# The first half product of the experts' first multiplication, passed on in PSUM

## The chip, the core and the metric

The kernel runs on one core of a Trainium2 chip. The metric is device time in microseconds (us). Five engines take part: TensorE (PE, with its weight loads PEld in a row of their own), VectorE (DVE), ScalarE (ACT), GpSimd (POOL) and SyncE (SP), which issues transfers. Each engine runs its own instructions in the order in which they were written for it, and waits where an operand is not ready.

## The reference, cut to what matters

```python
x = attention(q, k, v, phi)                # 4 x 8 x 576 x 64, as [2304, 512]
h = x @ w_in;  x = (h * cos(h)) @ w_out    # [512, 2048], [2048, 512]
p = domain_probs / (domain_probs.sum(-1, keepdims=True) + 1e-09)
out = 0
for e in range(4):
    h = maximum(x @ w1[e], 0.0)            # [2304, 512] @ [512, 1024]
    out += p[:, e:e+1] * (h @ w2[e])       # [2304, 1024] @ [1024, 512]
```

All values are 32-bit floats. The change touches the product `x @ w1[e]` in the last loop.

## The kernel before, in words

The kernel has two stages. The first (to about 374 us of the profiled execution) computes attention and the product with `w_in` and `w_out`; its order is written out word by word in a plan. The second stage is the loop over experts. It takes the 2304 tokens in two halves, the weights in 16 slices of 256 columns of `w1` (four per expert), and each half's 1152 tokens in two sub-blocks, of 2 x 256 and 2 x 320 tokens. That makes 64 units, one after the other: half by half, within a half slice by slice, within a slice the two sub-blocks.

Every number is held as a sum of a high and a low part, and a product of two such numbers takes three products on TensorE (`mm3`): high by high, high by low, low by high. All products are recorded under line L342.

**A unit's first multiplication** (`hidden`). The block `x @ w1` is a 2 x 2 by 2 x 2 block multiplication done with seven block products instead of eight (in the manner of Strassen and Winograd). The mixed blocks of x are made by `build_x`, once for each half and sub-block: DVE or POOL forms sums and differences in `sA`, `sB` and `acc` (line L390), ACT copies them into the high part (`x<-sB`, line L373), DVE or POOL forms the low part. The mixed blocks of `w1` lie in `wa`. Each of the seven products is six instructions on TensorE, `hp<-x,wa`, 256 or 320 columns wide. They go into three PSUM banks, `px`, `py` and `pz`, all named `hp` in the profile:

- the first product goes into `px`, the fifth into `py`, the second into `pz`;
- ACT copies `px` to SBUF as `p1` (named `p` in the profile, `p<-hp`), and DVE adds `pz` and `p1` into `c` (`c<-hp,p`, line L1089): the first quarter of the result;
- the sixth product adds itself onto `px`, ACT copies it as `u2`; the seventh adds itself, ACT copies it as `u3` (both are `u<-hp` in the profile); the fourth adds itself: the second quarter;
- DVE adds `py` and `u3` into `c`: the third quarter. The third product adds itself onto `py`, and DVE adds `py` and `u2`: the last quarter.

So the sixth product waits for the copy `p1`, the seventh for `u2`, the fourth for `u3`.

**The relu** (`rectify`) reads `px` and `c` with ACT, and writes `c` or a tile `ht` (`h`, `hg` or `hx` in the profile, whose low part DVE makes, L1092). **A unit's second multiplication** takes tokens in tiles of 128, most of them in pairs (`pair_prep`, `pair_out`), the others singly (`one_prep`, `plain_out`). POOL or DVE mix the relu's result in `sm`, ACT copies it into `h7` (the high part). The products `op<-wb,h` and `op<-wt,h` go into two banks `op` for a pair, three instructions of 256 columns each. After the first and the sixth product of a pair DVE gathers (`acc<-op,p_all`, lines L1101 and L1103: weighted by p, added to the output in `acc`); the next product adds itself onto the same bank and waits for the gather. In the second half the first of these gathers of a pair is a copy `ev` on ACT, added to `acc` by POOL or DVE.

**Banks.** `px`, `py` and `pz` come from a ring of four PSUM banks (`p`); `op` comes from another of four (`po`). A unit gives `pz` back after the sum `c<-hp,p`, `px` after the relu, `py` after the last sum. Units 0 and 1 take `pz` from the ring `po`.

**The order.** All steps of the second stage are generators; a list scheduler (`Order.run`) holds estimated times for every engine and hands out the next instruction by estimated start and rank. An instruction's place on its engine is thus decided by estimates when the kernel is written, and the engine keeps to it.

## Time and profile before

| what | value |
|---|---|
| three runs | 1119.89, 1120.53, 1120.99 us; median 1120.53 |
| span of the profiled execution | 1118.8 us |
| from that span to the median of the runs | 1.7 us |
| TensorE busy | 1109.8 us, 99% |
| VectorE busy | 879.0 us, 79% |
| ScalarE busy | 583.7 us, 52% |
| GpSimd busy | 668.5 us, 60% |

The span runs from the first to the last instruction of one profiled execution; the runs' times are taken from outside and hold a little more. A busy share says how long an engine worked, not whether anything waited for it. A row of the timeline has the start, the time from the first start to the last end, engine, line, operation, output and inputs, partitions by elements, and how many instructions were merged (x); what stands in brackets is idle time ahead of it and what ended that. Matmuls overlap: the next one starts before the one ahead has ended, so a group's pace is read from start to start.

### The profile page before, as it was taken

What the parts mean: (1) busy time and instruction counts of PE and PEld (TensorE: products, weight loads), DVE (VectorE), ACT (ScalarE), POOL (GpSimd) and SP (SyncE); (2) the same over time, 40 slices, a digit from 0 to 9 for tenths busy, and PEclk for the clock granted to TensorE, in tenths of its full rate; (3) what the DMA queues carried; (4) which work ended last, traced back from release to release, by engine and by line L of the source; (5) the groups of instructions that cost most, each with busy time, mean ns of one, the idle gap of its engine ahead of it and who ended that gap; (6) DMA issues with size and microseconds to landing.
All of it is one profiled execution on the core that took longest, in us unless ns stands there. A gap on an engine that the chain in (4) does not pass through costs nothing.

```text
span 1118.8 us, 22424 instructions
## 1 busy us (share of the span) xinstructions
PE 1109.8 (99%) x8698; PEld 1055.6 (94%) x8698; DVE 879.0 (79%) x1619; ACT 583.7 (52%) x1219; POOL 668.5 (60%) x1001
## 2 busy tenths in 40 slices
PE   9899999999999999999999999999999999999998
PEld 8689999999999989999999999989999999999997
DVE  5888988898888765777888888778777777777776
ACT  4887766565655424444444543445455545554543
POOL 1455556665677404665767664217587877777774
PEclk9999999999999999999999999999999999999999
DMA  9940636167614037443566456683554345434532
GB/s 305 359 137 25 213 129 228 57 227 266 254 39 180 1 118 250 161 161 114 186 253 237 181 181 232 247 337 130 191 205 174 142 167 214 185 142 154 215 131 86
DMA packets 44299, 201.76 MB, mean 180 GB/s; under 512 B 6176, under 2 KB 15392, under 8 KB 29984
## 3 DMA queue, kind: packets, MB, share of 16 engines
q1 hardware_dynamic: 44192, 200.33, 49.1%
q8 instruction: 68, 1.11, 0.4%
q14 instruction: 39, 0.32, 0.1%
HBM read 132.68 MB, written 67.63 MB: 179 GB/s over the span
## 4 chain that ended last, share of the span: by engine, by line
PE 97%; DMA 1%; DVE 1%; SPq 0%; ACT 0%; issue 0%
PE op L342 52%; PE hp L342 41%; DMA q<-in_qt_dram 1%; PE vw_ps L629 1%; PE warm L765 1%; PE kvp L513 1%; PE spare L757 1%; PE sc L566 0%; SPq L370 0%; PE pe L487 0%; DVE st L576 0%; PE pkt L535 0%; DVE sA L390 0%; ACT u L373 0%; DVE stT L596 0%
## 5 line engine op out<-in xcount | busy, mean ns | idle before, releaser
L342 PE MATMUL hp<-x,wa 128*128 128x320 f32 (+1 forms) x2688 | 405.7, 296 | 0.7 <-ACT u L373 0.5
L1103 DVE SCALAR_TENSOR_TENSOR acc<-op,p_all,acc 128x256 f32<-128x256 f32 (+1 forms) x566 | 301.9, 566 | 121.6 <-PE op L342 117.3
L342 PEld LDWEIGHTS hp<-x,wa 128*128 128x128 f32 x2688 | 373.6, 188 | 5.7 <-ACT u L373 1.2
L342 PE MATMUL op<-gt,wo 128*128 128x288 f32 x1536 | 218.1, 296 | 0.0
L342 PEld LDWEIGHTS op<-gt,wo 128*128 128x128 f32 x1536 | 208.1, 188 | 4.5 <-issue 2.4
L390 POOL TENSOR_TENSOR sm<-c 128x128 f32<-128x128 f32 x180 | 88.2, 496 | 157.6 <-ACT c L373 156.5
L342 PE MATMUL op<-wb,h 128*128 128x256 f32 (+1 forms) x786 | 144.7, 298 | 0.0
L342 PE MATMUL op<-wt,h 128*128 128x256 f32 x888 | 143.3, 281 | 0.0
L373 ACT ACTIVATE u<-hp 128x320 f32<-128x320 f32 (+1 forms) x128 | 52.6, 411 | 154.3 <-PE hp L342 154.3
L342 PEld LDWEIGHTS op<-wt,h 128*128 128x128 f32 x888 | 124.7, 189 | 2.4
L342 PEld LDWEIGHTS op<-wb,h 128*128 128x128 f32 x786 | 116.8, 189 | 3.9
L342 PE MATMUL op<-wb,hg 128*128 128x512 f32 (+1 forms) x477 | 115.5, 385 | 0.0
L342 PE MATMUL hp<-attnT,vw 128*128 128x288 f32 x768 | 113.2, 296 | 0.2 <-DVE attnT L390 0.2
L342 PEld LDWEIGHTS hp<-attnT,vw 128*128 128x128 f32 x768 | 105.2, 188 | 3.5 <-issue 1.6
L390 POOL TENSOR_TENSOR gt<-y,gt 128x576 fp32r<-128x576 f32 x41 | 60.0, 1463 | 79.1 <-ACT gt L373 74.7
L342 PEld LDWEIGHTS op<-wb,hg 128*128 128x128 f32 x477 | 84.8, 188 | 15.5
L736 DVE TENSOR_TENSOR acc<-op,acc 128x576 f32<-128x576 f32 (+1 forms) x120 | 84.7, 710 | 18.6 <-PE op L342 17.3
L390 POOL TENSOR_TENSOR h<-c,h 128x128 fp32r<-128x128 f32 (+1 forms) x140 | 84.3, 621 | 15.8 <-ACT h L373 15.8
L1089 DVE TENSOR_TENSOR c<-hp,u 128x320 f32<-128x320 f32 (+1 forms) x128 | 57.9, 452 | 33.5 <-PE hp L342 24.5
L373 ACT ACTIVATE kk<-hp 128x576 int32<-128x576 f32 x64 | 41.6, 650 | 45.2 <-PE hp L342 45.0
L373 ACT ACTIVATE h<-sm 128x512 fp32r<-128x512 f32 x74 | 46.6, 629 | 34.4 <-POOL sm L390 34.3
L373 ACT ACTIVATE c<-c 128x256 f32<-128x256 f32 (+1 forms) x138 | 55.2, 434 | 14.9 <-DVE c L1089 14.9
(144 smaller groups left out, 1644.8 us busy)
## 6 DMA issues: line engine op xcount, KB each, us to landing
wa<-wa_d SPq DMA_DIRECT2D x21, 1792.0 KB, 8.7
wa_d<-wa SPq DMA_DIRECT2D x16, 1792.0 KB, 10.3
wt<-wt_d SPq DMA_DIRECT2D x21, 1024.0 KB, 4.9
wb<-wb_d SPq DMA_DIRECT2D x21, 1024.0 KB, 7.0
raw<-in_w_dram SPq DMA_DIRECT2D x32, 512.0 KB, 4.9
wt_d<-wt SPq DMA_DIRECT2D x16, 1024.0 KB, 7.3
wb_d<-wb SPq DMA_DIRECT2D x16, 1024.0 KB, 6.7
kv<-in_kv_dram SPq DMA_DIRECT2D x16, 512.0 KB, 7.9
```

Source lines behind the costliest of these rows:

```text
L342: nc.tensor.matmul(out=ps, lhsT=lt(a), rhs=rt(b), start=first and i == 0, stop=last and i == 2, skip_group_check=more,)
L373: return Op("ACT", ns, fn or (lambda: nc.scalar.activation(out=out, in_=in_, func=func, **kw)), *deps, table=table)
L390: eng.tensor_tensor(out=out, in0=in0, in1=in1, op=op)
L513: nc.tensor.matmul(out=kvp[32 * i:32 * i + 32], lhsT=es[:n, c, 32 * i:32 * i + 32], rhs=kv[i // 2][0][0][:, c, i % 2] if c < NC else kv[i ...
L629: nc.tensor.matmul(out=ps[32 * i:32 * i + 32, g, j * FS:j * FS + FS], lhsT=kvT[b][64 * g:64 * g + 64, 1, i, :], rhs=wi[s][0][64 * g:64 * g ...
L736: e = yield dve(155 + 301 * nd, lambda: nc.vector.tensor_tensor(out=dst, in0=op[:, :, :TH], in1=dst, op=ALU.add), o)
L757: nc.tensor.matmul(out=bank, lhsT=ones, rhs=ones, start=True, stop=True, skip_group_check=True)
L765: nc.tensor.matmul(out=warm[:, :128], lhsT=ones, rhs=ones, start=True, stop=True)
L1089: return dve(157 + 1.045 * n, lambda: nc.vector.tensor_tensor(out=out, in0=ps, in1=sb, op=ALU.add), *deps)
L1103: nc.vector.scalar_tensor_tensor(out=dst, in0=ps, scalar=pe, in1=dst, op0=ALU.mult, op1=ALU.add)
```

## The change

In 61 of the 64 units (all but those listed in `PLAIN_SUM`) ACT copies `px` into a PSUM bank of its own, `z`, in place of the SBUF tile `p1`. The second product then adds itself onto that copy (`more=True` leaves out the clearing of the bank), after the sixth. DVE's sum is gone, and the relu reads `z`. The ring `p` has three banks instead of four, and `z` is one bank with a ring of its own. Units 0 and 1 still take `pz` from `po`, unit 2 from `z` now. The diff:

```diff
@@ -138,8 +138,9 @@
 FIRST = "00 01 10 11 02 12 03 13".split()
 PAIRS = ((0,), (1,), (2, 3), (4, 5), (6, 7))
 RINGS = dict(phi=3, kv=4, q=4, raw=2, wi=2, wf=1, wo=2, es=2, st=2, stT=1, kvs=1, vw=2, y=2, kk=1, gt=3, h=2, o=2, c=2,
-             p2=2, raw2=2, tt=1, wa=2, wb=2, wt=2, cq=2, p1=2, u2=2, u3=1, ht0=1, ht1=1, h7=4, h7a=2, h7f=3, h1a=1, sma=2, h1=1, sm=2, p=4, po=4, ev=4, eva=2)
+             p2=2, raw2=2, tt=1, wa=2, wb=2, wt=2, cq=2, p1=2, u2=2, u3=1, ht0=1, ht1=1, h7=4, h7a=2, h7f=3, h1a=1, sma=2, h1=1, sm=2, p=3, z=1, po=4, ev=4, eva=2)
 HALVES = (0,)
+PLAIN_SUM = (0, 1, 2)
 MERGED = ()
 PATIENCE = ({"PE": 0.2, "ACT": 0.5, "DVE": 0.5, "POOL": 0.5, "SP": 0.5, "X": 0.0},
             {"PE": 0, "ACT": 0, "DVE": 0, "POOL": 0.5, "SP": 0.5, "X": 0.0},
@@ -1054,7 +1055,8 @@
     h_ctx = ExitStack()
     h_p = [h_ctx.enter_context(tc.tile_pool(name="hg", bufs=1, reuse_waits="tile"))]
     p_ctx.close()
-    ps_p = ctx.enter_context(tc.tile_pool(name="ps_p", bufs=4, space=PSUM, reuse_waits="tile"))
+    ps_p = ctx.enter_context(tc.tile_pool(name="ps_p", bufs=3, space=PSUM, reuse_waits="tile"))
+    ps_z = ctx.enter_context(tc.tile_pool(name="ps_z", bufs=1, space=PSUM, reuse_waits="tile"))
     ps_q = ctx.enter_context(tc.tile_pool(name="ps_q", bufs=4, space=PSUM, reuse_waits="tile"))
 
     PROD = {1: (0, 0), 2: (1, 1), 3: (2, 2), 4: (6, 3), 5: (3, 4), 6: (4, 5), 7: (5, 6)}
@@ -1252,6 +1254,10 @@
             return pe(6 * max(0.4545 * n + 0.5, 119.5), 130, prod(bank, i_, more), *deps)
 
         def bank(ring="p"):
+            if ring == "z":
+                if not zs:
+                    zs.append(ps_z.tile([128, 512], F32, tag="z", name="z", bufs=1))
+                return zs[0]
             return (ps_p if ring == "p" else ps_q).tile([128, 512], F32, tag="p" if ring == "p" else "q", name="hp")
 
         def kept(tag):
@@ -1264,18 +1270,24 @@
         ky, t0 = yield R["p"]
         py = bank()
         o5 = yield mm(py, 5, t0)
-        k1, t1 = yield R["p1"]
-        p1 = kept("p1")
-        a1 = yield a_(n, p1, px[:, :n], ACTF.Copy, o1, t1)
-        rz = "po" if i < 2 else "p"
+        rz = "po" if i < PLAIN_SUM[-1] else "z"
         kz, t0 = yield R[rz]
         pz = bank(rz)
         todo.set(("H?", i), None)
-        o2 = yield mm(pz, 2, t0)
-        o6 = yield mm(px, 6, a1, more=True)
-        c11 = yield sum_(n, c[:, 0, :n], pz[:, :n], p1, o2, a1, tc_)
-        R[rz].give(kz, c11)
-        R["p1"].give(k1, c11)
+        if i in PLAIN_SUM:
+            k1, t1 = yield R["p1"]
+            p1 = kept("p1")
+            a1 = yield a_(n, p1, px[:, :n], ACTF.Copy, o1, t1)
+            o2 = yield mm(pz, 2, t0)
+            o6 = yield mm(px, 6, a1, more=True)
+            c11 = yield sum_(n, c[:, 0, :n], pz[:, :n], p1, o2, a1, tc_)
+            R[rz].give(kz, c11)
+            R["p1"].give(k1, c11)
+            pz = None
+        else:
+            a1 = yield a_(n, pz[:, :n], px[:, :n], ACTF.Copy, o1, t0)
+            o6 = yield mm(px, 6, a1, more=True)
+            c11 = yield mm(pz, 2, a1, more=True)
         k2, t1 = yield R["u2"]
         u2 = kept("u2")
         a2 = yield a_(n, u2, px[:, :n], ACTF.Copy, o6, t1)
@@ -1287,7 +1299,7 @@
         c22 = yield sum_(n, c[:, 1, n:], py[:, :n], u3, o5, a3, tc_)
         R["u3"].give(k3, c22)
         last = pe(6 * max(0.4545 * n + 0.5, 119.5), 130, prod(py, 3, True), c22)
-        mids[i] = c, kc, px, kx, py, ky, u2, k2, a2, o4, c11, c22, last, tc_
+        mids[i] = c, kc, px, kx, py, ky, pz, kz, u2, k2, a2, o4, c11, c22, last, tc_
         todo.set(("mid", i), None)
         o3 = yield last
         todo.set(("H", i), o3)
@@ -1298,14 +1310,17 @@
         u, s, j = units[i]
         n = SUBS[j][1]
         yield have(("mid", i))
-        c, kc, px, kx, py, ky, u2, k2, a2, o4, c11, c22, o3, tc_ = mids.pop(i)
+        c, kc, px, kx, py, ky, pz, kz, u2, k2, a2, o4, c11, c22, o3, tc_ = mids.pop(i)
+        top = c[:, 0, :n] if pz is None else pz[:, :n]
         if mode(i) != "whole":
             r = yield a_(n, c[:, 0, n:], px[:, :n], ACTF.Relu, o4, tc_)
             R["p"].give(kx, r)
             r2 = yield a_(n, c[:, 1, n:], c[:, 1, n:], ACTF.Relu, c22)
             cs_[i] = c, kc
             todo.set(("c", i, 1), Join([r, r2]))
-            r3 = yield a_(n, c[:, 0, :n], c[:, 0, :n], ACTF.Relu, c11)
+            r3 = yield a_(n, c[:, 0, :n], top, ACTF.Relu, c11, tc_)
+            if pz is not None:
+                R["z"].give(kz, r3)
             yield have(("H", i))
             c12 = yield sum_(n, c[:, 1, :n], py[:, :n], u2, o3, a2, tc_)
             R["u2"].give(k2, c12)
@@ -1317,6 +1332,9 @@
         if through:
             r = yield a_(n, c[:, 0, n:], px[:, :n], ACTF.Relu, o4, tc_)
             R["p"].give(kx, r)
+            if pz is not None:
+                c11 = yield a_(n, c[:, 0, :n], top, ACTF.Relu, c11, tc_)
+                R["z"].give(kz, c11)
             yield have(("H", i))
             c12 = yield sum_(n, c[:, 1, :n], py[:, :n], u2, o3, a2, tc_)
             R["u2"].give(k2, c12)
@@ -1346,8 +1364,10 @@
         h = yield a_(n, ht[:, 0, 0, n:2 * n], px[:, :n], ACTF.Relu, o4, th)
         l1 = yield low_(n, ht[:, 1, 0, n:2 * n], px[:, :n], ht[:, 0, 0, n:2 * n], h, psum=True)
         R["p"].give(kx, l1)
-        h = yield a_(n, ht[:, 0, 0, :n], c[:, 0, :n], ACTF.Relu, c11, th)
-        l2 = yield low_(n, ht[:, 1, 0, :n], c[:, 0, :n], ht[:, 0, 0, :n], h)
+        h = yield a_(n, ht[:, 0, 0, :n], top, ACTF.Relu, c11, th)
+        l2 = yield low_(n, ht[:, 1, 0, :n], top, ht[:, 0, 0, :n], h, psum=pz is not None)
+        if pz is not None:
+            R["z"].give(kz, l2)
         yield have(("H", i))
         c12 = yield sum_(n, c[:, 1, :n], py[:, :n], u2, o3, a2, tc_)
         R["u2"].give(k2, c12)
```

The line numbers of the changed kernel are one higher in the first stage's code and two or more higher behind it (L342 is L343 there, L1103 is L1105). By instruction, TensorE has as many products as before, DVE 54 instructions fewer, ACT 2 more, POOL 7 fewer. The order is the same through the whole first stage.

**Place A, the first two units of the second stage.** These are TensorE's instructions from unit 0's second product on, before. `hp_5014`, `hp_5031` and `hp_5040` are unit 0's `px`, `py` and `pz`; `hp_5042`, `hp_5065` and `hp_5084` are unit 1's; `wa_3732` and `wa_3931` are their slices.

```order
L342 MATMUL hp_5040<-x_4709,wa_3732 128x256 x6
L342 MATMUL hp_5014<-x_4708,wa_3732 128x256 x6
L342 MATMUL hp_5042<-x_4708,wa_3931 128x256 x6
L342 MATMUL hp_5065<-x_4710,wa_3931 128x256 x6
L342 MATMUL hp_5014<-x_4711,wa_3732 128x256 x6
L342 MATMUL hp_5084<-x_4709,wa_3931 128x256 x6
L342 MATMUL hp_5042<-x_4708,wa_3931 128x256 x6
L342 MATMUL hp_5014<-x_4712,wa_3732 128x256 x6
L342 MATMUL hp_5031<-x_4709,wa_3732 128x256 x6
L342 MATMUL hp_5042<-x_4711,wa_3931 128x256 x6
L342 MATMUL hp_5042<-x_4712,wa_3931 128x256 x6
L342 MATMUL op_5142<-wb_4223,hg_5109 128x512 x6
```

And the same place in the changed kernel, where the six names are `hp_5017`, `hp_5034`, `hp_5041`, `hp_5044`, `hp_5099` and `hp_5110`.

```order
L343 MATMUL hp_5041<-x_4709,wa_3732 128x256 x6
L343 MATMUL hp_5017<-x_4708,wa_3732 128x256 x6
L343 MATMUL hp_5044<-x_4708,wa_3931 128x256 x6
L343 MATMUL hp_5017<-x_4711,wa_3732 128x256 x6
L343 MATMUL hp_5017<-x_4712,wa_3732 128x256 x6
L343 MATMUL hp_5034<-x_4709,wa_3732 128x256 x6
L343 MATMUL hp_5099<-x_4710,wa_3931 128x256 x6
L343 MATMUL hp_5110<-x_4709,wa_3931 128x256 x6
L343 MATMUL hp_5044<-x_4708,wa_3931 128x256 x6
L343 MATMUL op_5122<-wb_4223,hg_5088 128x512 x6
```

Unit 0's sixth, seventh and fourth product moved ahead of unit 1's fifth and second; and unit 1's fifth and second stand behind unit 0's last product. ACT's instructions of this stretch, before:

```order
L373 ACTIVATE p1_5038<-hp_5014 128x256
L373 ACTIVATE u2_5058<-hp_5014 128x256
L373 ACTIVATE x_5020<-sB_5023 128x640
L373 ACTIVATE p1_5074<-hp_5042 128x256
L373 ACTIVATE u3_5082<-hp_5014 128x256
L373 ACTIVATE x_5019<-sA_5022 128x640
```

And in the changed kernel:

```order
L374 ACTIVATE p1_5042<-hp_5017 128x256
L374 ACTIVATE u2_5061<-hp_5017 128x256
L374 ACTIVATE x_5023<-sB_5026 128x640
L374 ACTIVATE u3_5076<-hp_5017 128x256
L374 ACTIVATE x_5022<-sA_5025 128x640
L374 ACTIVATE hg_5088<-hp_5017 128x256
```

The copy `u3` of unit 0 stands directly behind the copy of `x` from `sB`, where unit 1's copy `p1` stood before.

**Place B, a single tile's products between two units.** These are TensorE's instructions before; `hp_5438` is a unit's `px`, `hp_5520` its `pz`, and `op_5541` and `op_5542` belong to a tile of the first unit.

```order
L342 MATMUL hp_5485<-x_5019,wa_5276 128x320 x6
L342 MATMUL hp_5520<-x_5016,wa_5276 128x320 x6
L342 MATMUL hp_5438<-x_5020,wa_5276 128x320 x6
L342 MATMUL op_5541<-wb_5406,hg_5109 128x256 x3
L342 MATMUL op_5542<-wb_5406,hg_5109 128x256 x3
L342 MATMUL op_5542<-wt_5194,hg_5109 128x256 x3
L342 MATMUL hp_5438<-x_5021,wa_5276 128x320 x6
```

And in the changed kernel, with `hp_5431` for the `px` and `z_5213` for the bank `z`.

```order
L343 MATMUL hp_5476<-x_5022,wa_5279 128x320 x6
L343 MATMUL hp_5431<-x_5023,wa_5279 128x320 x6
L343 MATMUL z_5213<-x_5019,wa_5279 128x320 x6
L343 MATMUL op_5537<-wb_5407,hg_5088 128x256 x3
L343 MATMUL hp_5431<-x_5024,wa_5279 128x320 x6
L343 MATMUL op_5538<-wb_5407,hg_5088 128x256 x3
L343 MATMUL op_5538<-wt_5217,hg_5088 128x256 x3
```

The second product moved behind the product of `px` that it stood ahead of, and the next product of `px` stands one `op` product earlier.

**Place D, the first pairs of the second half.** TensorE's instructions before; `op_9403` is a pair's first bank, `hp_9469` a `px`, `hp_9488` a `py`, `hp_9501` a `pz`.

```order
L342 MATMUL op_9347<-wt_8962,h7_9306 128x256 x3
L342 MATMUL op_9348<-wb_9213,h7_9306 128x256 x3
L342 MATMUL op_9403<-wt_8962,h7_9325 128x256 x2
L342 MATMUL op_9403<-wt_8962,h7_9326 128x256
L342 MATMUL hp_9469<-x_9176,wa_9077 128x320 x6
L342 MATMUL hp_9488<-x_9180,wa_9077 128x320 x6
L342 MATMUL hp_9501<-x_9177,wa_9077 128x320 x6
L342 MATMUL op_9403<-wt_8962,h7_9325 128x256 x2
L342 MATMUL op_9403<-wt_8962,h7_9326 128x256
L342 MATMUL hp_9469<-x_9181,wa_9077 128x320 x6
```

In the changed kernel at the same pair, whose banks are `op_9328` and `op_9329` here; `op_9274` and `op_9275` are those of the pair ahead, `op_9400` and `op_9401` those of the first pair whose first gather is a copy `ev`, and `hp_9426` is the next unit's `px`.

```order
L343 MATMUL op_9275<-wb_9130,h7_9217 128x256 x3
L343 MATMUL op_9328<-wt_8892,h7_9242 128x256 x2
L343 MATMUL op_9328<-wt_8892,h7_9243 128x256
L343 MATMUL op_9328<-wt_8892,h7_9242 128x256 x2
L343 MATMUL op_9328<-wt_8892,h7_9243 128x256
L343 MATMUL op_9329<-wb_9130,h7_9242 128x256 x2
L343 MATMUL op_9329<-wb_9130,h7_9243 128x256
L343 MATMUL op_9400<-wb_9278,h7_9354 128x256 x3
L343 MATMUL op_9401<-wb_9278,h7_9354 128x256 x3
L343 MATMUL op_9401<-wt_8897,h7_9354 128x256 x3
L343 MATMUL op_9400<-wt_8897,h7_9354 128x256 x3
L343 MATMUL hp_9426<-x_9100,wa_8988 128x320 x6
```

The hp products that stood between a pair's first product and the next one on the same bank have gone from there. DVE's gathers that these products wait for, and what follows them there, in the changed kernel:

```order
L1103 TENSOR_SCALAR acc_70<-op_9328,p_all_78 128x256
L1103 TENSOR_SCALAR acc_70<-op_9274,p_all_78 128x256
L1105 SCALAR_TENSOR_TENSOR acc_70<-op_9275,p_all_78,acc_70 128x512
L1103 TENSOR_SCALAR acc_70<-op_9328,p_all_78 128x256
L1105 SCALAR_TENSOR_TENSOR acc_70<-op_9329,p_all_78,acc_70 128x256
L1103 TENSOR_SCALAR acc_70<-op_9328,p_all_78 128x256
L1105 SCALAR_TENSOR_TENSOR acc_70<-op_9329,p_all_78,acc_70 128x512
L391 TENSOR_TENSOR x_9101<-acc_70,x_9101 128x640
L391 TENSOR_TENSOR sB_9108<-acc_70,sB_9108 128x640
```

The two instructions of `build_x` (`x_9101` and `sB_9108`) stand behind all gathers of that pair. On ACT before, around the first copy `ev`:

```order
L373 ACTIVATE h7_9474<-c_9253 128x256
L373 ACTIVATE h7_9474<-c_9253 128x128
L373 ACTIVATE h7_9474<-sm_9305 128x512
L373 ACTIVATE u2_9526<-hp_9469 128x320
L373 ACTIVATE ev_9534<-op_9511,p_all_78 128x256
L373 ACTIVATE u3_9562<-hp_9469 128x320
```

And in the changed kernel:

```order
L374 ACTIVATE h7_9374<-c_9161 128x256
L374 ACTIVATE h7_9374<-c_9161 128x128
L374 ACTIVATE h7_9374<-sm_9216 128x512
L374 ACTIVATE x_9102<-sB_9108 128x640
L374 ACTIVATE ev_9427<-op_9400,p_all_78 128x256
L374 ACTIVATE z_5213<-hp_9426 128x320
```

Between the copies `h7` and the copy `ev` there now stands the copy of `x_9102` from `sB_9108`, and the copy into `z` stands behind `ev`.

## Rows read from the trace of the kernel before

**Rows 1.** Busy time, share of the span and instructions by engine (the page).

```profile
PE 1109.8 (99%) x8698; PEld 1055.6 (94%) x8698; DVE 879.0 (79%) x1619; ACT 583.7 (52%) x1219; POOL 668.5 (60%) x1001
```

**Rows 2.** Idle time of TensorE's weight loads by releaser: us, times, longest.

```profile
PEld hp L342 <- ACT u L373: 1.2, 3, 0.7
```

**Rows 3.** Timeline of TensorE, last stage: start, duration, rows merged (x).

```profile
904.26 1.60 PE L342 MATMUL hp<-x,wa 128*128 128x256 f32 x12
905.70 0.52 PE L342 MATMUL op<-wt,h 128*128 128x256 f32 x3
```

**Rows 4.** Timeline of TensorE around its four late spots, second stage.

```profile
383.82 4.85 PE L342 MATMUL hp<-x,wa 128*128 128x256 f32 x36
389.14 0.97 PE L342 MATMUL hp<-x,wa 128*128 128x256 f32 x6 [0.47 <-ACT u L373]
...
437.44 0.52 PE L342 MATMUL op<-wt,hg 128*128 128x256 f32 x3
437.90 1.15 PE L342 MATMUL hp<-x,wa 128*128 128x320 f32 x6
...
760.63 0.51 PE L342 MATMUL op<-wb,h 128*128 128x256 f32 x3
761.26 0.98 PE L342 MATMUL hp<-x,wa 128*128 128x256 f32 x6
...
1104.81 1.71 PE L342 MATMUL op<-wt,h 128*128 128x256 f32 x12
1106.36 0.52 PE L342 MATMUL op<-wb,h 128*128 128x256 f32 x3
```

**Rows 5.** Groups of instructions: the removed sum and the copy before it.

```profile
L1089 DVE TENSOR_TENSOR c<-hp,p 128x256 f32<-128x256 f32 (+1 forms) x64 | 28.7, 448 | 6.0 <-PE hp L342 5.2 <-issue 0.3 <-POOL hx L390 0.2
L373 ACT ACTIVATE p<-hp 128x256 f32<-128x256 f32 (+1 forms) x64 | 25.6, 400 | 29.1 <-PE hp L342 29.1
```

**Rows 6.** Timeline of all engines at the start of the second stage.

```profile
380.94 7.72 PE L342 MATMUL hp<-x,wa 128*128 128x256 f32 x60
383.62 0.81 DVE L390 TENSOR_TENSOR sB<-sA,acc 128x640 f32<-128x640 f32 x1
384.47 0.74 ACT L373 ACTIVATE x<-sB 128x640 fp32r<-128x640 f32 x1 [1.50 <-DVE sB L390]
385.11 0.36 ACT L373 ACTIVATE p<-hp 128x256 f32<-128x256 f32 x1
387.27 0.38 ACT L373 ACTIVATE hg<-hp 128x256 fp32r<-128x256 f32 x1 [0.34 <-PE hp L342]
387.68 0.42 DVE L1092 SCALAR_TENSOR_TENSOR hg<-hp,hg 128x256 fp32r<-128x256 f32 x1 [0.22 <-ACT hg L373]
```

**Rows 7.** Timeline of ACT ahead of the late spot at 437.9.

```profile
436.90 0.63 ACT L373 ACTIVATE h<-sm 128x512 fp32r<-128x512 f32 x1 [2.65 <-POOL sm L390]
437.44 0.42 ACT L373 ACTIVATE u<-hp 128x320 f32<-128x320 f32 x1
```

**Rows 8.** Timeline of TensorE and DVE, end of the first half's units.

```profile
720.79 4.60 PE L342 MATMUL hp<-x,wa 128*128 128x320 f32 x30
725.23 1.56 PE L342 MATMUL op<-wb,hx 128*128 128x512 f32 x6
721.66 0.41 DVE L1092 SCALAR_TENSOR_TENSOR hx<-hp,hx 128x256 fp32r<-128x256 f32 x1
```

**Rows 9.** Timeline of DVE and ACT where the second half's units begin.

```profile
766.93 0.48 DVE L1101 TENSOR_SCALAR acc<-op,p_all 128x256 f32<-128x256 f32 x1
767.32 0.74 DVE L1103 SCALAR_TENSOR_TENSOR acc<-op,p_all,acc 128x512 f32<-128x512 f32 x1
764.96 0.73 ACT L373 ACTIVATE x<-sB 128x640 fp32r<-128x640 f32 x1
771.51 0.47 ACT L373 ACTIVATE ev<-op,p_all 128x256 f32<-128x256 f32 x1
```

More of the change, by code (lines that the diff above doesn't have):

```diff
@@ L1359, in rectify @@
         todo.set(("ht", i), Join([l1, l2, l3]))
-    mids = {}
+    mids, zs = {}, []
     cs_, hts, hx, hg, sma, mixed, full = {}, {}, [], [], [], [], []
```

## The prediction

> **What bounds the kernel now.** I read the busy shares first: TensorE works 99% of the span, DVE 79%, ACT 52% [rows 1]. So nothing that lightens DVE or ACT shortens the run by itself; only TensorE's lost time counts. Next I looked for what TensorE loses in the second stage, which is all the change touches. The list of waits shows its weight loads idle 1.2 us in three waits for a copy `u`, the longest 0.7 [rows 2], and no larger wait for this stage's products. The timeline gives the pace: twelve 256-column products take 1.44 us, 0.12 each [rows 3], thirty 320-column ones 4.44, 0.148 each [rows 8]. Against that pace four spots are late [rows 4]: 36 products from 383.82 to 389.14 take 5.32 instead of 4.32 (1.0 lost), the three at 437.44 take 0.46 instead of 0.36, the three at 760.63 take 0.63, the twelve at 1104.81 take 1.55 instead of 1.44. Behind a wait the next six lose 0.1 more (0.97 and 0.98 long where twelve take 1.60, so six 0.88). Together: 1.1 + 0.2 + 0.37 + 0.1, some 1.8 us. That is all the second stage can give back, 0.16% of the time. What the change is worth is therefore decided by the waits that its new order makes.
>
> **The change, part by part.** The sum `c<-hp,p` costs DVE 448 ns [rows 5]; 61 of 64 go, 27.3 us of DVE. It stands beside TensorE's work (no late spot names it), so it is worth nothing directly. The copy stays, 61 times, but into PSUM. No row shows ACT writing PSUM; the nearest is the same copy into SBUF, 400 ns [rows 5], and I take that. From below: shorter gains nothing, as the copy is covered. From above: with 0.1 more it is late only where no more than six 256-column products (0.72) stand between the first product and the sixth, three places, at 0.2 each: 0.6. The Trainium skill (ScalarE: Activation LUTs, Step-by-step: what each stage is for) says that ScalarE reaches PSUM sooner than SBUF; no run here shows that yet, and by it the upper end falls away and the sum below stays. TensorE's number of products is the same, and a second product that adds itself is like the sixth and seventh, which already do. The relu then reads the bank instead of `c`, one ACT pass as before.
>
> What costs is the order. The second product no longer stands between the fifth and the sixth, and a unit has three rotating banks and `z` instead of four rotating ones. I went through the waits of TensorE in the new order and priced each by rows. A copy that ends is followed by its product 0.04 later (437.44 + 0.42 = 437.86, product at 437.90) [rows 4, 7].
>
> Place A, start of the stage. Sixty hp products run in one piece from 380.94 [rows 6]. In the new order the fifth group of six is unit 0's fourth product, wanted at 380.94 + 24 x 0.12 = 383.82. It needs `u3`, and on ACT `u3` stands right behind the copy of x from `sB`, where `p` stood. That copy waits for DVE's `sB` (383.62, 0.81 long) and starts at 384.47; the copy behind it starts at 385.11 and ends 385.47 [rows 6]. DVE's order up to `sB` is unchanged. So the product starts at 385.51, 1.69 late. The third product follows at 386.23 but needs a DVE sum that stands behind the 0.81 subtraction of x: about 386.45, 0.25 late. Unit 1's fifth product now needs unit 0's bank: the copy `hg<-hp` and DVE's subtraction take 0.83 from start to end (387.27 to 388.10 [rows 6]) after the fourth product, with another x subtraction between: 0.3 late. With 0.1 behind each: 2.5 us, where 1.1 were lost: +1.4 (0.5 to 2.0).
>
> Place B, the spot at 437.90. The seventh product there waits for a `u` copy that stands on ACT behind `h<-sm` (436.90), itself waiting for POOL [rows 7]. ACT's order there is the same, but six 256-column products (0.72) move behind the seventh product. It is wanted at 437.08 and starts at 437.90: 0.82 + 0.1, where 0.2 were lost: +0.7 (0.3 to 0.8).
>
> Place C, the first half's last units. The second group of the thirty products from 720.79, at 721.68, is a fifth product; with three rotating banks it needs the bank that DVE's `hx<-hp` reads until 721.66 + 0.41 = 722.07 [rows 8]. It starts at 722.11: 0.43 + 0.1, +0.5 (0 to 0.8). Before, the third group needed that bank, at 722.57.
>
> Place D, where the second half's units begin. Before, three groups of hp stand between the products of a pair; in the new order the pair products follow one another, each waiting for a gather on DVE. Count from the start of the op_9328 products that open the new TensorE excerpt's second row. DVE's first gather of its excerpt is done by then. A 256-wide gather lasts 0.48 and the next starts 0.39 after it, a 512-wide one lasts 0.74 [rows 9]. So gather 2 starts at -0.13, the wide one at 0.26, gather 4 at 0.93, done 1.41. TensorE wants it at 0.36 and starts at 1.45: 1.09 late. The next gather ends at 1.9, TensorE asks at 1.81: 0.1 late. Nine products more to 3.37, then one needs the copy `ev`. DVE has two more gathers, x (0.81 like `sB`) and `sB` to 4.64; ACT copies x from `sB` (0.73) to 5.41 and only then `ev` (0.47) [rows 6, 9]: 5.88. So 2.5 late. Together 3.7 + 0.3, where 0.37 were lost: +3.6 (1.0 to 5.0: from below the `ev` wait gone, from above one gather and one subtraction more ahead of it). Queued behind `ev` on ACT is the copy into `z`, wanted a microsecond later.
>
> Place E: six times in the last 290 us a pair product follows its gather with only six 256-column products between. Such a place cost 0.11 at 1104.81 [rows 4]; six less the one that goes: +0.6 (0 to 0.8).
>
> Sum: 1.4 + 0.7 + 0.5 + 3.6 + 0.6 = 6.8 us, bounds 1.8 to 9.4 (10.0 with the copies' 0.6). The profiled execution spans 1118.8; 1.7 us lie around it up to the median of 1120.5. On the span that gives 1125.6, on the median 1127.3. Where DVE's 27.3 us go: into idle time. The last products and gathers stand as before, so the end costs the same. Every load of x and weights keeps at least 7 us of products, at the pace above, between itself and its use.
>
> **The rivals.** *No change.* DVE, lighter by 61 sums, reaches the two `sB` mixes sooner than its order says. Decisive at D: `sB` must end 2.5 us earlier, before TensorE asks for `ev`. Then A and D lose what they lost before and B, C, E remain: 1.8 us, 1122.3, inside 0.2% (2.2 us). For it speaks DVE's share; against it, that at A no sum is gone yet (units 0 and 1 keep theirs) and at D gathers fill the queue. *Faster.* All 1.8 us of today's late spots vanish: 1118.7, still within 0.2%; more would have to come from outside the stage. *Bank bound.* Place C repeats in every one of the 61 units, 0.43 each: 26 us, 1146.8. In the steady stage the new order leaves 2 us of products or more, at the pace above, between the last reader's release and the bank's next product, which speaks against it. The Trainium skill (Perfetto Trace Analysis, Optimizing Tensor Performance, Matmuls) asks that independent groups of products rotate through different banks, so that one's evacuation overlaps the next; by that rule three banks in place of four cost time. The trace agrees at place C alone, with 0.43.
>
> **How the numbers follow.** My sum 0.77, no change 0.15, faster 0.03, bank bound 0.05. A measurement of this kernel tells 0.2%, 2.2 us, from nothing. The predicted time is 1127.3. The range reaches from the no-change case, 1121.9, to the upper bound 1120.5 + 9.4 = 1129.9; about 0.12 is left out below and above. Slower 0.81 (0.77 and 0.05, less 0.01 for a sum at its lowest bounds), same 0.15, faster 0.04.
>
> **What would show it.** In the changed profile: TensorE's weight loads idle several us on `u`, `ev`, gathers and `hg`, against 1.2; a wait of 1.7 near 384, 0.8 near 437, 0.4 near 722, 1.1 and 2.5 near 770; copies into `z` of 0.36 to 0.44; DVE's busy time some 20 us less. If the waits near 770 are missing, D is wrong, most likely because DVE's order there runs ahead. If hp waits for `z` or a bank in the steady stage, the bank rival holds.

## The result, and the profile after

The changed kernel takes 1130.66 us, the median of four runs (1129.58 to 1132.98), where the kernel before took 1120.76 beside it: a ratio of 1.0092, with a 95% interval from 1.0079 to 1.0105. That is 9.9 us more. The prediction said 1127.3 and slower, with a range to 1129.9: the direction was right, the time lies 0.8 us above the range.

The profiled execution spans 1127.3 us. The page's first part, which answers to [rows 1]:

```profile
PE 1113.7 (99%) x8698; PEld 1057.9 (94%) x8698; DVE 857.4 (76%) x1565; ACT 586.8 (52%) x1221; POOL 659.3 (58%) x994
```

DVE is busy 21.6 us less, TensorE's busy time has grown by 3.9 although it has the same 8698 instructions: some of them are recorded as longer. The list of waits of TensorE's weight loads answers to [rows 2] (us in total, times, longest):

```profile
PEld op L343 <- ACT ev L374: 3.3, 1, 3.3
PEld hp L343 <- ACT u L374: 2.6, 2, 1.7
PEld op L343 <- DVE acc L1103: 1.0, 1, 1.0
PEld hp L343 <- DVE hx L1094: 0.6, 1, 0.6
```

Before there was one row of this size in the stage, 1.2 us, for `u`. Now one wait for `ev` alone takes 3.3. The timeline shows the five places of the prediction in order of time; compare the start of a row with the start of the one ahead plus its number of instructions at full pace (0.12 for 256 columns, 0.147 for 320).

```profile
380.05 3.05 PE L343 MATMUL hp<-x,wa 128*128 128x256 f32 x24
384.64 4.41 PE L343 MATMUL hp<-x,wa 128*128 128x256 f32 x30 [1.53 <-ACT u L374]
...
383.58 0.74 ACT L374 ACTIVATE x<-sB 128x640 fp32r<-128x640 f32 x1 [1.51 <-DVE sB L391]
384.22 0.36 ACT L374 ACTIVATE u<-hp 128x256 f32<-128x256 f32 x1
...
437.10 0.51 PE L343 MATMUL op<-wb,hg 128*128 128x256 f32 x3
438.26 1.15 PE L343 MATMUL hp<-x,wa 128*128 128x320 f32 x6 [0.65 <-ACT u L374]
...
722.15 1.05 PE L343 MATMUL hp<-x,wa 128*128 128x320 f32 x6
723.49 1.74 PE L343 MATMUL hp<-x,wa 128*128 128x320 f32 x10 [0.29 <-DVE hx L1094]
...
768.67 0.62 PE L343 MATMUL op<-wt,h 128*128 128x256 f32 x3
770.11 0.62 PE L343 MATMUL op<-wt,h 128*128 128x256 f32 x3 [0.82 <-DVE acc L1103]
771.79 0.52 PE L343 MATMUL op<-wt,h 128*128 128x256 f32 x3
771.96 1.54 DVE L391 TENSOR_TENSOR x<-acc,x 128x640 fp32r<-128x640 f32 x1
773.43 0.81 DVE L391 TENSOR_TENSOR sB<-acc,sB 128x640 f32<-128x640 f32 x1
774.27 0.74 ACT L374 ACTIVATE x<-sB 128x640 fp32r<-128x640 f32 x1 [1.20 <-DVE sB L391]
774.91 0.46 ACT L374 ACTIVATE ev<-op,p_all 128x256 f32<-128x256 f32 x1
775.42 0.62 PE L343 MATMUL op<-wt,h 128*128 128x256 f32 x3 [3.12 <-ACT ev L374]
775.88 3.00 PE L343 MATMUL hp<-x,wa 128*128 128x320 f32 x12
778.67 0.84 PE L343 MATMUL op<-wt,h 128*128 128x256 f32 x3
...
844.46 0.88 PE L343 MATMUL hp<-x,wa 128*128 128x256 f32 x6
845.22 0.62 PE L343 MATMUL op<-wt,h 128*128 128x256 f32 x3
```

At A 24 products from 380.05 should end at 382.93 by pace, and the next starts at 384.64: 1.71 late, as worked out (1.69). The two ACT rows show why: the copy `u` stands behind the copy of x, whose start waited for `sB`. At B the product follows 1.16 after a group of 0.36: 0.80 late. At C it is 1.34 after a group of 0.88: 0.46 late. At D the gather costs 1.44 - 0.36 = 1.08, with the 0.1 that products lose behind a wait (the fill), and the wait for `ev` 775.42 - 771.79 - 0.36 = 3.27. At E a group of six takes 0.76 where 0.72 is the pace, 0.15 with the fill behind it, and this stands six times.

Behind the wait for `ev` the next rows are slow themselves: twelve products of 320 columns from 775.88 to 778.67 take 2.79, not 1.76. The view by stretches, with its heading (PEclk is the granted clock as a share of full speed), shows it:

```profile
core 0: us, PE busy (x) PEld busy (x) DVE busy (x) ACT busy (x) POOL busy (x), PEclk, DMA share, GB/s
771.50:775.50 4.00, 0.89 (x8) 0.68 (x7) 3.53 (x5) 1.73 (x3) 1.38 (x5) 1.00 0.01 4
775.50:780.00 4.50, 4.50 (x22) 4.50 (x23) 2.81 (x6) 0.42 (x1) 0.96 (x1) 0.62 0.00 0
780.00:784.00 4.00, 4.00 (x31) 4.00 (x31) 1.33 (x4) 1.35 (x3) 0.00 (x0) 1.00 0.00 0
```

TensorE worked 0.89 of the 4 us before; then its granted clock is 0.62 on the mean of 4.5 us, a stretch at the lower level (1.2 GHz; a product of 320 columns follows the one ahead by 0.267 there) and the rest at 2.4. By 780 it is back at 1.00. Counted start to start, the products there take 1.5 us more than at full pace.

The new copy answers to [rows 5]:

```profile
L374 ACT ACTIVATE z<-hp 128x320 f32<-128x320 f32 x31 | 13.1, 422 | 37.6 <-PE hp L343 35.9 <-DVE hx L1094 1.7
L374 ACT ACTIVATE z<-hp 128x256 f32<-128x256 f32 x30 | 11.0, 367 | 13.7 <-PE hp L343 9.0 <-DVE hg L1094 4.7
```

The copy into PSUM takes 422 and 367 ns (320 and 256 columns). The old copy into SBUF took 430 and 369 in the same view of the kernel before. The 400 ns of the prediction were right. The Trainium skill (ScalarE: Activation LUTs, Step-by-step: what each stage is for) says that ScalarE reaches PSUM sooner than SBUF; here that is worth 2 to 8 ns, so by the measurement it doesn't matter in this kernel.

### The profile page after: what moved, and what is told of

The parts are those of the page before. It is cut to its first block, busy times and chain, and to the rows that moved or that the text cites. A ratio compares the mean times of both kernels' runs of the same rounds, so it can differ in the third digit from the quotient of the medians.

```text
span 1127.3 us, 22364 instructions
## 1 busy us (share of the span) xinstructions
PE 1113.7 (99%) x8698; PEld 1057.9 (94%) x8698; DVE 857.4 (76%) x1565; ACT 586.8 (52%) x1221; POOL 659.3 (58%) x994
## 4 chain that ended last, share of the span: by engine, by line
PE 96%; DMA 2%; DVE 1%; SPq 0%; ACT 0%; POOL 0%; issue 0%; POOLq 0%
PE op L343 52%; PE hp L343 36%; PE z L343 4%; PE vw_ps L630 1%; DMA kv<-in_kv_dram 1%; DMA q<-in_qt_dram 1%; PE warm L766 1%; PE kvp L514 1%; SPq L371 0%; PE sc L567 0%; DVE x L391 0%; DVE acc L1105 0%; PE spare L758 0%; POOL hg L391 0%; DVE sB L391 0%
## 5 line engine op out<-in xcount | busy, mean ns | idle before, releaser
L1105 DVE SCALAR_TENSOR_TENSOR acc<-op,p_all,acc 128x256 f32<-128x256 f32 (+1 forms) x566 | 302.9, 568 | 141.0 <-PE op L343 138.2
L343 PE MATMUL hp<-x,wa 128*128 128x256 f32 (+1 forms) x2316 | 356.0, 297 | 2.6 <-ACT u L374 2.2
L343 PEld LDWEIGHTS hp<-x,wa 128*128 128x128 f32 x2316 | 324.1, 189 | 7.3 <-ACT u L374 2.6
L343 PE MATMUL op<-gt,wo 128*128 128x288 f32 x1536 | 218.1, 296 | 0.0
L343 PEld LDWEIGHTS op<-gt,wo 128*128 128x128 f32 x1536 | 208.1, 188 | 4.6 <-issue 2.4
L391 POOL TENSOR_TENSOR sm<-c 128x128 f32<-128x128 f32 x180 | 85.4, 478 | 181.6 <-ACT c L374 181.5
L343 PE MATMUL op<-wt,h 128*128 128x256 f32 x888 | 143.0, 282 | 3.9 <-ACT ev L374 3.1
L343 PE MATMUL op<-wb,h 128*128 128x256 f32 (+1 forms) x786 | 141.3, 299 | 0.0
L343 PEld LDWEIGHTS op<-wt,h 128*128 128x128 f32 x888 | 124.3, 189 | 7.5 <-ACT ev L374 3.3
L343 PEld LDWEIGHTS op<-wb,h 128*128 128x128 f32 x786 | 114.9, 189 | 3.9
L343 PE MATMUL op<-wb,hg 128*128 128x512 f32 (+1 forms) x477 | 115.1, 385 | 0.0
L343 PE MATMUL hp<-attnT,vw 128*128 128x288 f32 x768 | 113.2, 296 | 0.3 <-DVE attnT L391 0.3
L343 PEld LDWEIGHTS hp<-attnT,vw 128*128 128x128 f32 x768 | 105.1, 188 | 3.5 <-issue 1.6
L343 PEld LDWEIGHTS op<-wb,hg 128*128 128x128 f32 x477 | 85.3, 188 | 15.9
L684 DVE SCALAR_TENSOR_TENSOR y<-hp,kk 128x576 f32<-128x576 f32 x64 | 48.1, 751 | 16.7 <-ACT kk L374 16.3
```

The lines of the kernel that those rows point to most:

```text
L343: nc.tensor.matmul(out=ps, lhsT=lt(a), rhs=rt(b), start=first and i == 0, stop=last and i == 2, skip_group_check=more,)
L391: eng.tensor_tensor(out=out, in0=in0, in1=in1, op=op)
L684: o = yield dve(750, lambda: nc.vector.scalar_tensor_tensor(out=y, in0=hv, scalar=0.25, in1=kk, op0=ALU.add, op1=ALU.subtract), o, t0)
L1105: nc.vector.scalar_tensor_tensor(out=dst, in0=ps, scalar=pe, in1=dst, op0=ALU.mult, op1=ALU.add)
```

## Where the time went

From the first product of the second stage to the last one's start it is 739.83 us before (374.72 to 1114.55) and 749.30 after (373.82 to 1123.12): 9.47 more. Counted from start to start, with what the next products lose behind each wait:

| place | before | after | more | predicted |
|---|---|---|---|---|
| A, 380 to 389 | 1.10 | 2.36 | 1.26 | 1.4 |
| B, 437 | 0.21 | 0.92 | 0.71 | 0.7 |
| C, 722 | 0 | 0.56 | 0.56 | 0.5 |
| D, waits at 761 and 768 to 776 | 0.38 | 4.73 | 4.35 | 3.6 |
| D, products at the lower clock | 0 | 1.53 | 1.53 | none |
| E, six gathers | 0.10 | 0.88 | 0.78 | 0.6 |
| four other spots of 0.07 to 0.09 | 0 | 0.31 | 0.31 | none |
| sum | 1.8 | 11.3 | 9.5 | 6.8 |

The runs add 0.5 us outside the span: those of the changed kernel take 2.25 us more than their spans, those of before 1.79. The first stage, whose order is the same, took 0.9 us less in this profiled execution; among the eight profiles of this document whose clock did not fall in it the second stage starts between 372.9 and 374.9, and no cause was looked for. Nor was one for the four other spots.

## The experiments

The theory is that only the new order costs time, at places A to E and by the clock behind D. Its rival is that the arithmetic (the copy into PSUM, the product that adds itself onto it, a bank fewer) costs in every unit. To part them, the order that the scheduler had made was written out as a list and followed word for word, so that arithmetic and order could be exchanged.

**The new order with the old sums (e1).** In the 61 units:

```diff
-            a1 = yield a_(n, pz[:, :n], px[:, :n], ACTF.Copy, o1, t0)
+            a1 = yield a_(n, p1, px[:, :n], ACTF.Copy, o1, t1)
             o6 = yield mm(px, 6, a1, more=True)
-            c11 = yield mm(pz, 2, a1, more=True)
+            o2 = yield mm(pz, 2, t0)
...
+    def add_up(i):
...
+        o = yield sum_(n, c[:, 0, :n], pz[:, :n], p1, o2, a1, tc_)
```

The sum is a step of its own (`add_up`), so that the written-out list can place it on DVE; `...` stands for lines left out.

> The order of the changed kernel on every engine, its three rotating banks and its one bank z, but the old arithmetic: ACT copies the first product to SBUF, the second product clears its bank, and DVE adds the two (61 sums come back, placed on DVE where their product ends). Theory (only the order of the instructions, the waits at A to E and the clock behind D, makes the change slower): the same waits stand, 1130.7 us, ratio 1.0092, within 0.0015. Rival (the copy into PSUM and the product that adds itself onto it cost time in each of 61 units, 0.16 us each): 1120.8 to 1122, ratio under 1.0015.

Measured: 1135.12 us, ratio 1.0136 (1.0123 to 1.0149). Its waits:

```profile
PEld hp L547 <- DVE c L1295: 3.9, 7, 0.7
PEld op L547 <- ACT ev L578: 2.9, 1, 2.9
PEld hp L547 <- ACT u L578: 2.6, 2, 1.7
PEld op L547 <- DVE acc L1309: 2.0, 4, 1.0
```

The waits for `u` and `ev` are nearly those of the changed kernel, as the theory says, so the old arithmetic doesn't mend them; the rival's 1120.8 to 1122 are far off. But the theory's 1130.7 was missed too, by 4.4 us: the sums, back on DVE, stand ahead of gathers and of the sums `c` that TensorE waits for, two rows that the changed kernel does not have in this size. In the new order, and placed like this, DVE's 61 sums are not free. The granted clock behind this kernel's wait for `ev` (2.9) stayed at 1.00, so a wait of nearly three microseconds did not bring the lower clock here.

**The old order with the new sum (e2).** The order of the kernel before, and in 61 units the copy into the second product's bank, and ACT's relu where DVE's sum stood:

```diff
+            a1 = yield a_(n, pz[:, :n], px[:, :n], ACTF.Copy, o1, t0)
+            todo.set(("H?", i), None)
+            o2 = yield mm(pz, 2, a1, more=True)
+            o6 = yield mm(px, 6, a1, more=True)
+            c11 = yield a_(n, c[:, 0, :n], pz[:, :n], ACTF.Relu, o2, tc_)
```

The lines that go are those of the change itself; `rectify`'s later relu of that quarter goes too. In this kernel some columns of the 320-wide units lose the first product; the number and the sizes of its instructions don't depend on that.

> The order of the kernel before on every engine and its four rotating banks, but the new arithmetic in 61 units: ACT copies the first product into the bank of the second, which adds itself; where DVE's sum stood, ACT applies the relu from that bank into c, and the later relu of that quarter is left out where there was one of its own. Theory (the order alone): 1120.8 us, ratio 1.000, up to 1.002 where the copy is late, since the second product now waits for it with only the fifth product (0.72 or 0.88 us) between. Rival (the arithmetic or the bank itself costs): 1129 to 1131, ratio about 1.009.

Measured: 1122.59 us, ratio 1.0025 (1.0015 to 1.0036), second stage 742.1 us, 2.3 more than before. Its waits beyond those of before:

```profile
PEld hp L546 <- ACT hp L577: 1.6, 4, 0.9
PEld hp L546 <- ACT u L577: 1.0, 2, 0.7
```

The second row is that of before [rows 2], with one place fewer. Four times the second product waits for the copy (`hp<-hp`), 1.6 us in all by the weight loads, with the fill behind them nearly the 2.3. That is a little over the 1.002 that the expectation allowed for late copies. The arithmetic itself costs nothing that can be seen in the other 57 units. The rival's 1129 is out.

**x of the second half earlier (e4).** The changed kernel, and one line:

```diff
-RX = (8, 305, 337)
+RX = (8, 295, 324)
```

> The changed kernel with two numbers of its order changed: the ranks of the two x blocks of the second half, 305 and 337, become 295 and 324, so that the scheduler hands their mixes out earlier. Arithmetic and banks are as in the changed kernel, and the order up to 700 us is too. Theory (place D costs 1.0 + 0.1 + 3.3 and 0.3 behind its waits, and 1.5 by the clock, 6.1 us together): no wait over 0.5 us near 770, granted clock 1.0 there, 1124.6 us, ratio 1.0035. Rival (the three banks or the arithmetic make the loss, and the idle time shows up elsewhere): 1128 or more.

Measured: 1123.35 us, ratio 1.0031 (1.0019 to 1.0043), second stage 742.95: 6.35 us less than the changed kernel, where 6.1 were expected. TensorE's largest wait for ACT is the one at A, 1.7 for `u`, and the same pairs run at pace, without `ev` or a gather in between:

```profile
768.03 0.88 PE L343 MATMUL op<-wb,h 128*128 128x256 f32 x6
768.74 0.88 PE L343 MATMUL op<-wt,h 128*128 128x256 f32 x6
769.46 1.05 PE L343 MATMUL hp<-x,wa 128*128 128x320 f32 x6
```

The granted clock is 1.00 throughout. So place D is two thirds of the whole loss, and it hangs on when two blocks of x are made, not on the sum.

**A bank for unit 1 as well (e5).** As e4, and

```diff
-        ky, t0 = yield R["p"]
-        py = bank()
+        ry = "z" if i == 1 else "p"
+        ky, t0 = yield R[ry]
+        py = bank(ry)
...
-            R["p"].give(ky, c12)
+            R["z" if i == 1 else "p"].give(ky, c12)
...
```

> As the run with the x blocks earlier (ranks 295 and 324), and the fifth product of unit 1 goes into bank z, idle then, so that it needs no bank of unit 0; the scheduler then hands out the first units as in the kernel before. Theory (place A is made by the ring of three: unit 1 waits for unit 0's bank, and unit 0's products move together): the wait of 1.70 us near 382 and its followers (2.3 us in all) go back to the 1.1 us of the kernel before, 1.2 us less than that run: ratio 1.002. Rival (place A comes from the copy of x alone): the wait stays, ratio 1.003.

Measured: 1122.80 us, ratio 1.0020 (1.0006 to 1.0034), second stage 741.66, 1.3 less than e4. At the start of the stage:

```profile
381.16 2.32 PE L343 MATMUL hp<-x,wa 128*128 128x256 f32 x18
383.32 0.88 PE L343 MATMUL z<-x,wa 128*128 128x256 f32 x6
384.04 4.84 PE L343 MATMUL hp<-x,wa 128*128 128x256 f32 x36
```

From 381.16 to 384.04 the 24 products take 2.88, the full pace; the 36 behind them lose the 1.0 of before [rows 4] (the next row starts at 389.35). The wait of 1.7 is gone. The time alone can't tell the theory's 1.002 from the rival's 1.003; the trace does: place A was made by the ring of three, which kept unit 1 from starting its fifth product and so drew unit 0's products together.

**All but C and E mended (e6).** As e5 with the first rank at 12; in the written-out order the copy `u` at B stands ahead of the copy of `sm`, and one product of unit 1 stands one place earlier.

> As the run before it, with the first x block's rank at 12, and three edits of the written-out order: at place B the copy u2 stands ahead of the copy of sm on ACT, in unit 1 one product stands one place earlier on TensorE. Places C (0.45 + 0.1) and E (six times 0.04 + 0.1) stay. Theory (places A, B and D are all else that the change costs, and DVE's 61 sums are worth nothing): TensorE loses about 2 us in the second stage, as before (1.8), ratio 1.000 to 1.0015. Rivals: the arithmetic costs in every unit, ratio 1.003 or more; or the lighter DVE gives something back, ratio under 0.999.

Measured: 1121.73 us against 1120.29 beside it, ratio 1.0005 (0.9993 to 1.0017): no difference that can be told. The second stage takes 740.60, 0.8 more than before. At B:

```profile
437.28 0.52 PE L545 MATMUL op<-wt,hg 128*128 128x256 f32 x3
438.00 0.62 PE L545 MATMUL op<-wt,hg 128*128 128x256 f32 x3 [0.20 <-DVE acc L1307]
```

0.72 where 0.36 is the pace: the wait for `u` is gone and a smaller one for a gather has come. C and E still cost 0.55 and 0.89; A, with its x block's new rank, loses 0.36 where before lost 1.1, and the wait of before at 761 (0.38) is gone. These partly cancel, which leaves the 0.8. With the four spots of 0.07 to 0.09 these places make up all that TensorE loses in this stage beyond before, so nothing larger is left for the changed arithmetic to cost or for the 61 sums fewer on DVE to gain.

**The wait filled (e3, e7).** The changed kernel in its own order, with products of ones into bank `z` ahead of the product that waits for `ev`: 24 in e3, 14 in e7 (which add themselves onto what lies there). The lines of e3:

```diff
+        if (i, k) == (33, 0):
+            yield pe(24 * 119.5, 130, lambda: [filler(zs[0][:, :128]) for _ in range(24)])
         m6 = yield prod(px, 4, 4, e1, more=True)
```

> The changed kernel in its own order with 24 products of ones (128 columns each, into bank z, which nobody uses there; their result is overwritten) ahead of the product that waits 3.3 us for ev at 772 us. Theory (the products behind that wait run at half pace because TensorE stood idle; they take 1.5 us more than at full pace): the granted clock stays at 1.0 behind the wait, the wait itself stays about 3.3 us with 2.9 of it filled, and the time is 1.5 us less than the changed kernel's, about 1129.2. Rival (the clock falls there whatever TensorE does, or its fall is chance): 1130.7, and the granted clock of 775.5 to 780 is again near 0.6.

In e3 one later unit loses the first product in part of its columns. Measured: 1133.48 us, ratio 1.0116 (1.0101 to 1.0131), where the theory said 1129.2. The time says nothing for or against the theory, for two reasons that the trace shows. The 24 products are 48 instructions of 0.11, 5.28 us, and outlast the wait by 2.0. And the clock fell elsewhere (the stretch around place A, and the one that holds D):

```profile
380.00:400.00 20.00, 18.46 (x114) 17.03 (x113) 15.45 (x26) 8.11 (x17) 1.30 (x1) 0.91 0.00 1
770.00:784.00 14.00, 13.17 (x110) 12.79 (x109) 10.93 (x20) 5.58 (x14) 8.65 (x15) 1.00 0.02 7
```

0.91 on the mean of 20 us stands behind the wait of 1.7 at A, which costs 3.5 with what follows it where it costs 2.34 to 2.37 in the other profiles that have it: 1.2 more. Behind D the clock is 1.00. A second fall stood in the first stage of this execution. Of the six profiles with the wait of 1.7 at A, this is the one in which the clock fell behind it; why is not known.

> The changed kernel in its own order with 14 products of ones in the wait for ev, in place of the 24 of the earlier run, which took 5.28 us (48 instructions of 0.11) and so outlasted the wait: 28 instructions, 3.1 us, within the wait of 3.3. They add onto columns of z that the next copy overwrites. Theory (the half pace behind the wait is TensorE's clock after standing idle): granted clock 1.0 from 775 to 780, the twelve products there at 0.147, 1.5 us less than the changed kernel run beside it, a ratio lower by 0.0014. Rival: the same clock near 0.6 there and the same time as the changed kernel.

Measured: 1127.95 us, ratio 1.0065 (1.0045 to 1.0085), beside the changed kernel's 1130.33 (e8). TensorE's timeline and the stretch behind the wait:

```profile
775.70 0.52 PE L545 MATMUL op<-wt,h 128*128 128x256 f32 x3
776.06 3.29 PE L1793 MATMUL z<-ones 128*128 128x128 f32 x28
779.15 0.62 PE L545 MATMUL op<-wt,h 128*128 128x256 f32 x3
779.61 1.93 PE L545 MATMUL hp<-x,wa 128*128 128x320 f32 x12
781.37 0.52 PE L545 MATMUL op<-wt,h 128*128 128x256 f32 x3
```

```profile
775.50:780.00 4.50, 4.50 (x41) 4.50 (x40) 4.03 (x6) 1.73 (x3) 2.60 (x4) 1.00 0.02 4
```

The twelve products from 779.61 to 781.37 take 1.76, the full pace, and the clock is 1.00. The group behind the wait still starts 3.45 after the one ahead, so the wait itself is that of e8. The second stage is 1.53 us shorter than in e8, the 1.5 that were expected. (The profiled execution is the slowest of its six, 1131.76: its first stage took 3.9 more than e8's, with a granted clock of 0.66 from 40 to 50.) The medians differ by 2.4, with intervals that overlap; 0.9 of it is not explained.

The clocks of all executions point the same way. The mean granted clock of the changed kernel is 0.997 or 0.998 in nine of its ten executions, that of e7 0.999 or 1.000 in five of six, that of e4, where the wait is gone, 1.000 in all six. So TensorE standing idle in this wait is what brings the lower clock behind it: filling the wait or taking it away keeps the clock up. It is not a rule for every wait of this length: behind e1's 2.9 the clock stayed up, and one execution of the changed kernel shows 1.000 and yet took 1129.27, no less than those at 0.998 beside it. Nor does every fall need it: five of the 23 executions of the kernel before, run beside e5 to e8, show 0.995 to 0.997.

**The changed kernel again (e8).**

> The changed kernel itself, beside the three others on one chip. Every theory: ratio 1.0092 within 0.0013, the wait for ev about 3.3 us, the clock near 0.6 for about 3 us behind it. A shorter wait for ev, or no fall of the clock, would say that the subtraction of x on DVE, 1.54 us in the first profile and 0.81 elsewhere, differs from run to run.

Measured: 1130.33 us, ratio 1.0084 (1.0062 to 1.0105).

```profile
771.83 0.52 PE L343 MATMUL op<-wt,h 128*128 128x256 f32 x3
775.28 0.63 PE L343 MATMUL op<-wt,h 128*128 128x256 f32 x3 [2.94 <-ACT ev L374]
775.75 3.19 PE L343 MATMUL hp<-x,wa 128*128 128x320 f32 x12
778.73 0.83 PE L343 MATMUL op<-wt,h 128*128 128x256 f32 x3
...
771.99 1.12 DVE L391 TENSOR_TENSOR x<-acc,x 128x640 fp32r<-128x640 f32 x1
773.02 1.07 DVE L391 TENSOR_TENSOR sB<-acc,sB 128x640 f32<-128x640 f32 x1
```

The wait is 775.28 - 771.83 - 0.36 = 3.09, 0.18 less than in the first profile, and twelve products take 2.98: the clock fell again. The subtraction of x does differ from run to run, 1.12 here, but the one of `sB` took 1.07 where it took 0.81: from the start of the first to the end of the second it is 2.10 here and 2.28 in the first profile, and that difference is the 0.18 of the wait.

## Why the prediction was right and wrong

**What bounds the kernel** held: TensorE does, and no gain could come from DVE. e6 shows it, with 61 sums fewer and the time of before.

**The price of the copy** (0.40, as into SBUF) held: 0.37 and 0.42. So did "the second product that adds itself is like the sixth": e2.

**Places A, B, C and E** held in place, cause and size: 1.26, 0.71, 0.56 and 0.78 us where 1.4, 0.7, 0.5 and 0.6 stood. e5 took A's wait away with a bank for unit 1, which puts the old order back there; e6 took B's wait for `u` away by moving the copy that was named as its cause, though a wait for a gather of about half the size came in its place. C and E are read from the trace alone, and no run took them away.

**Place D** is the step that failed. The chain of events was right: a gather 0.98 late where 1.09 was worked out, then `ev` behind x and `sB`. But the sum gave 3.6 with an upper bound of 5.0, and the place measured 5.9: one price in it was too small and one was put at nothing. The small one is the subtraction of x on DVE, priced at 0.81 "like `sB`", from a row where POOL stood idle. Here it took 1.54 (POOL was computing in the first 0.9 of it), and the wait for `ev` grew from 2.5 to 3.3; in e8 the same two subtractions shared the extra time otherwise, and the wait was 3.1. The price put at nothing is the clock: the prediction charged a wait with its length and the 0.1 behind it. TensorE's clock fell behind the long one, and the next 15 products or so paid 1.5 us more. In the profile of before, no wait in this stage is over 0.7 and the clock stays at 1.00 up to TensorE's last product, so no row of before had this price; the bounds could not hold it.

The table's sum is 2.7 us over the forecast 6.8, and place D holds 2.3 of that. Without the lower clock alone the time would have been about 1129.1, inside the range; e7, which keeps the wait and fills it, measured 1127.95. A measured 0.14 under its forecast and E 0.18 over, which cancel in the sum.

Two ends of the range do not follow from the prediction's own numbers. Its upper bound of the sum was 10.0 with the copies' 0.6, but the range took 9.4; with 10.0 it would reach 1130.5, and 1130.66 is still above. Its lower end, 1121.9, is called the no-change case, which the text puts at 1122.3.

**The rivals.** No change: DVE did not reach `sB` sooner, since gathers filled its queue up to 771.96, as argued. The bank as a bound in all units: C alone, as argued; the 0.43 beside "the trace agrees" was worked out from rows of before, and the changed profile shows 0.46 there. Faster: not seen; e6, with C and E left in, gains nothing either.

**Where DVE's freed time went**: "into idle time" was half the truth. In the new order the freed 27 us keep the gathers on time: e1, which puts the sums back on DVE where their products end, loses 4.5 us more.

## What to carry to other kernels

When an engine at 99% decides, an edit that relieves another engine is worth only what it does to the order, so read the new order for each wait before counting what was removed. A scheduler's ranks are tuned for one set of costs: two numbers (e4) were worth 6.35 us, more than three times the 1.8 that the second stage had to give back. And a long wait of TensorE can cost more than its length: here 3.1 to 3.3 us of waiting took 1.5 more from the products behind it in both profiles of the changed kernel, and 2.9 in e1 took nothing more. So give such a wait a second price and a range that holds it.

## What was not expected of the hardware

The subtractions on DVE with two SBUF inputs (`x<-acc,x` and `sB<-acc,sB`, 128x640) took 0.81 to 0.83 wherever POOL stood idle. At place D, where POOL was computing beside them, `x<-acc,x` took 1.54, 0.88, 1.13, 1.12 and 1.12 in the changed kernel, e1, e3, e7 and e8. `sB<-acc,sB` behind it took 0.81 in the first of these, where POOL had stopped by then, and 1.07 in the four others. The Trainium skill (SBUF — State Buffer, Who interferes with whom) says that a DVE instruction with two SBUF inputs contends with a GpSimd instruction that reads SBUF; the trace agrees at this place, though not everywhere: in e4 an `x<-acc,x` at 758.26 took 0.81 with POOL's `h<-c,h` beside it. The price of x differs by 0.43 between two executions of the same kernel. What decides it stays open. So does what makes the runs of kernels that write `z` 0.2 to 0.6 us longer around their span (2.0 to 2.4, before 1.79; e2, which has no bank of that kind, 1.78).
